# Batch 1's second product as seven half products, in a fused attention and mixer kernel on one core

## The chip, the core and the metric

The kernel runs on one core of a Trainium2 chip. Five engines work from queues of their own, each strictly in order: TensorE (PE in the profile; its weight loads are PEld), VectorE (DVE), ScalarE (ACT), GpSimd (POOL) and SyncE (SP), which only issues transfers. A semaphore holds an instruction, and with it all that stands behind it on its engine, until others are done. The metric is the device time of one execution in microseconds (us); lower is better.

## The reference

```python
q_p, k_p = phi(q), phi(k)             # relu(x) times cos and sin of the position, side by side
kv = einsum('bhsf,bhsd->bhfd', k_p, v);  z = k_p.sum(axis=2)
x  = (q_p @ kv) / (q_p . z + 1e-6)    # per head; heads joined: 8 batches x 576 x 512
u  = x + (x.T @ U @ V).T              # U 576x32, V 32x576, along the sequence
out = u + relu(u @ w_ch1) @ w_ch2     # w_ch1 512x2048, w_ch2 2048x512
```

q, k, v have 8 batches, 8 heads, 576 positions and 64 features; output is float32. The products run in bf16 with float32 sums in PSUM.

## The kernel before

The 576 positions of a batch are 4 chunks (c = 0 to 3) of 128 and a tail of 64; the tails of two batches (a pair, pr) make one chunk, cc=4. The first product u @ w_ch1 is done for 16 tiles j of 128 hidden columns: `g1_main` (L570) does four matmuls of 512 columns into one PSUM bank (g_ps), and ScalarE's relu (L589) writes `hid[b][:, j]`. `g1_tail` (L712) does the same for a tail chunk.

The second product has two forms. `g2_part` (L737) takes one chunk: 16 matmuls of 512 columns in four parts of four into one bank (o_ps, L762), then one VectorE add of u (L772) and a store. `half_part` (L865) takes two chunks, n and n+2, with the 2048 x 512 weights cut into four quarters `W2` (L796): instead of eight products of quarters it does seven (k = 0 to 6, product numbers in `ORDER`), each 8 matmuls of 256 columns into half a bank (h_ps, L894). It needs sums of hidden blocks made by `hid_sum` (L823, VectorE, L836; the fourth is done right after product 2) and sums of weight quarters made by `w2_sum` (L801, VectorE, L807, eight half sums). In the form "with g" the products alternate with units of a first product; in the form "alone", before this change used for batch 7 only, ScalarE copies products 1, 5, 6 and 4 out of PSUM (L912 to L920), VectorE adds products 2, 3 and 7 (L850), and GpSimd adds u and the copies (L921, L924).

The order is written out by hand. `slots` is a list of TensorE pieces; `put(at, f)` (L1346) hangs work behind slot `at`, and the loop at L1553 runs slot by slot, so that each engine's queue follows this order. Slots 0 to 15 are the first product of batch 0, 16 to 31 the second product of its four chunks, 32 to 47 the first product of batch 1, 48 to 51 the first product of the tail of batches 0 and 1, 52 to 55 the second product of that tail, 56 to 71 the second product of batch 1's four chunks (cc = 5 to 8) and 72 to 87 the first product of batch 2. The attention of batch b is hung in by `attention_plan` (L1007) around a slot w in `PLAN` (L998): q and k preparation (`q_prep`, `k_prep`), transpositions of q issued by SyncE (`qtr_dma`, L392), `kv_unit` (L340) at w and w+2, the five `x_unit` or `x_two` (L416, L1293: matmuls, a reciprocal and scalings) from w+4, `A_unit` and `u_mm` (L446, L476: the product with U and V), four `u_add` (L484, j = 0 to 3) and transpositions of u (`utr_dma`, L522). For batches 1 and 3, x_two has its scaling done by eight ScalarE copies (L1314).

PSUM has eight banks: X takes two, T one, and g0, g1, g2, o0, o1 one each. `Banks` (L55) deals them out in turn: tag "g" from g0, g1, g2, tag "o" from o0, o1, whoever asks next. `spare(at)` (L989) says which tag a piece of attention takes in a slot: "o" from 32 to 51, "g" from 52 on, and from 72 or 88 on other ones. Half products take banks from `ring` (L838), `bank(i)` being the i-th after `turn`. A piece that is given a bank waits until what was last written there has been read.

Stores of batch 0 and 1 that would crowd SyncE's queue are kept in `late` (L735) and issued behind slots 65 and 92 (L1551).

Of the kernel before, what the change touches and what calls it, by code (L numbers as in the profile page):

```python
# [17 lines left out]
def kernel(  # L18
# [53 lines left out]
    ps = Banks()  # L72
# [62 lines left out]
    V_, A_, G_ = nc.vector, nc.scalar, nc.gpsimd  # L135
# [599 lines left out]
    late = {}  # L735

    def g2_part(pr, cc, part, half=None):  # L737

        last = pr == NPAIR - 1 and cc == 4
        if part == 0 and not half or last and part == 3:  # L740
            if pr > 0:
                o_ps[pr, cc] = tail_bank()
            else:
                tag, bufs = ("g", 3) if 2 <= cc < 4 else ("o", 2)
                o_ps[pr, cc] = ps.tile([P, DM], FP32, tag=tag, bufs=bufs, name="o_ps")
        o = o_ps[pr, cc]
        if cc == 4:
            b, lhs, c = None, hid_tl[pr], 0
            u = u_tl[pr].rearrange("p (j n) -> p j n", n=P)
        else:  # L750
            b, c = (2 * pr, cc) if cc < 4 else (2 * pr + 1, cc - 5)
            lhs, u = hid[b], u_bf[b][:, :, c, :]

        if last:
            cols = slice(0, 384) if part < 3 else slice(384, DM)
            js = (range(0, 5), range(5, 10), range(10, NJ), range(NJ))[part]
        else:
            cols, js = slice(0, DM), range(part * 4, part * 4 + 4)
            if half is not None:
                js = js[2 * half : 2 * half + 2]  # L760
        for j in js:
            nc.tensor.matmul(  # L762
                out=o[:, cols],
                lhsT=lhs[:, j, c * P : c * P + P],
                rhs=w2_bf[:, j, cols],
                start=(j == 0),
                stop=(j == NJ - 1),
            )
        if js[-1] < NJ - 1:
            return  # L770
        o_sb = pool.tile([P, DM], FP32, tag="o_sb", bufs=8, name="o_sb")
        nc.vector.tensor_tensor(  # L772
            out=o_sb[:, cols].rearrange("p (j n) -> p j n", n=P),
            in0=u[:, cols.start // P : cols.stop // P, :],
            in1=o[:, cols].rearrange("p (j n) -> p j n", n=P), op=ALU.add,
        )
        eng = nc.gpsimd if pr < NPAIR - 1 else nc.scalar if part == 3 and last else nc.sync
        if pr == 0 and cc < 8:
            eng = nc.sync

        def store():
            if cc == 4:
                tail_store(eng, pr, o_sb, cols)
                return
            eng.dma_start(
                out=out[b].rearrange("(m k) n -> m k n", k=9)[:, c : c + 6 : 5, cols],
                in_=o_sb[:, cols],
            )

        if pr == 0 and cc < 7:  # L790
            late.setdefault(92 if 0 < cc < 5 else 65, []).append(store)
            return
        store()

# [6 lines left out]
    def w2_sum(n, half):  # L801

        a, b = (
            (W2[1], W2[0]), (W2[3], w2_s[0]), (W2[3], W2[1]), (W2[2], w2_s[1])
        )[n]
        js = slice(4 * half, 4 * half + 4)
        V_.tensor_tensor(  # L807
            out=w2_s[n][:, js], in0=a[:, js], in1=b[:, js], op=ALU.subtract
        )
# [28 lines left out]
    ring, turn = ["o0", "o1"], [0]  # L838
# [148 lines left out]
    ORD = (4, 0, 1, 2, 3)  # L987

    def spare(at):  # L989
        if at < 72:  # L990
            return ("o", 2) if 32 <= at < 52 else ("g", 3)
        return ("o", 2) if at < 88 else ("s", 1)

# [1 line left out]
    QORD = (4, 0, 1, 2, 3)  # L997
    PLAN = {  # L998
        2: (46, -15, V_, V_, -10, (-5, -4, -1)),
        3: (64, -12, V_, A_, -7, (3, 3, 18)),  # L1000
        4: (100, (-20, 1, V_, V_), (-13, 2, A_, V_), -12, (-9, -4, -4)),
        5: (127, (-24, 2, A_, A_), (-14, 2, A_, V_), (-14, -8, -5), (-8, -4, -4)),
        6: (157, (-23, 2, A_, A_), (-14, 2, A_, V_), (-14, -8, -6), (-8, -4, -4)),
        7: (189, (-24, 2, A_, A_), (-14, 2, A_, V_), (-12, -10, -8), ()),
    }

    def attention_plan(b):  # L1007

        plan = []
        if b < 4:  # L1010
            w, f_at, q_eng, k_eng, qtr, lo = PLAN[b]
        else:
            w, q_at, k_at, qtr, lo = PLAN[b]

        def put(at, f, *a, tag=False):
            if tag:
                a = a + spare(w + at)
            plan.append((w + at, lambda: f(b, *a)))

        for n, c in enumerate(QORD):  # L1020
            if b > 3:
                put(q_at[0] + q_at[1] * n, q_prep, c, q_at[2:])
                put(k_at[0] + k_at[1] * n, k_prep, c, k_at[2:])
                put(k_at[0] + (3 * n) // 2, v_prep, 0, H, (c,), (G_,))
                continue
            if b == 3:
                q_eng, k_eng = V_ if n == 3 else A_, A_ if n < 3 else None
                put((-12, -11, -10, -7, -3)[n], q_prep, c, (q_eng, q_eng))
                put(n - 9 if n < 3 else -5, k_prep, c, (A_, k_eng))
                if n > 2:  # L1030
                    put(2 * n - 12, k_prep, c, (None, V_))
                put(-4 if n > 2 else -6, v_prep, 0, H, (c,), (A_ if n > 2 else G_,))
                continue
            put(f_at + ((n - 1) % 5 if b == 2 else n), q_prep, c, (q_eng, q_eng))
            put(f_at + 6 + n, k_prep, c, (k_eng, k_eng))
            put((-6, -2, -1, -5, -5)[n], v_prep, 0, H, (c,), (V_ if n > 2 else A_,))
        for n, (c0, c1) in enumerate(((4, 5), (0, 2), (2, 4))):
            at = qtr[n] if b > 4 else 1 if b == 3 and n == 2 else qtr + 2 * n
            put(at, qtr_dma, c0, c1)
        plan.append((w + (b == 2), lambda: kv_unit(b, 0, *spare(w), A_ if b > 2 else V_)))  # L1040
        plan.append((w + 2, lambda: kv_unit(b, 1, *spare(w + 2), A_ if b > 2 else V_)))
        for n, c in enumerate(ORD):
            if b > 3:
                put((3 if b == B - 1 else 4) + 2 * n, x_unit, c, "X", 1)
            elif n % 2:
                put(9 if (b, n) == (3, 3) else 4 + (3 * n) // 2, x_two, c, tag=True)
            else:
                put(4 + (3 * n) // 2, x_unit, c, "X", 1)
        a_at = 15 - b if b < 4 else 14
        if b == B - 1:  # L1050
            put(a_at, A_unit, "s", 1, A_)
        else:
            put(a_at, A_unit, tag=True)
        odd = b % 2 == 1


        def two(at):
            return [T1, ("s", 1)] if at >= 88 else [spare(at)] * 2

        if b == B - 1:  # L1060
            plan.append((w + a_at + 2, lambda: u_mm(b, ("s", 1), js=(0, 1, 2))))
            plan.append((w + a_at + 5, lambda: u_mm(b, js=(3,))))
        else:
            plan.append((w + a_at + 2, lambda: u_mm(b, *two(w + a_at + 2))))
        for j in range(4):
            put(a_at + 2 + j + (2 if b > 4 and j > 1 else 0), u_add, j)
        put(a_at + 3, utr_dma, 0, 2)
        put(a_at + (7 if b > 4 else 5), utr_dma, 2, 4)
        if odd:
            if b == B - 1:  # L1070
                plan.append((w + a_at + 9, lambda: u_tail(b // 2, ("s", 1), js=(0, 1, 2))))
                plan.append((w + a_at + 11, lambda: u_tail(b // 2, js=(3,))))
            else:
                at = w + a_at + (10 if b == 5 else 9)
                plan.append((at, lambda at=at: u_tail(b // 2, *two(at))))
            put(a_at + (11 if b > 4 else 10), utr_dma, 4, 5)
        for at, t in zip(lo, loads(b + 1) if lo else ()):
            plan.append((w + at, t))
        return plan
# [44 lines left out]
    T1 = ("T", 1)  # L1124
# [219 lines left out]
    slots, todo = [], {}  # L1344

    def put(at, thunk):  # L1346
        todo.setdefault(at, []).append(thunk)

    def sums(b, n, ats):
        for i, at in enumerate(ats):  # L1350
            put(at, lambda i=i: hid_sum(b, n, i + 1))
# [24 lines left out]

    slots += [g1_second] + [g1(1, j) for j in range(1, NJ)]
    tail_slots(0)
    slots += [lambda cc=cc, p=p: g2_part(0, cc, p) for cc in range(4, 9) for p in range(4)]
    slots += [g1(2, j) for j in range(NJ)]  # L1380
    put(len(slots) - 1, lambda: ps.give("g", ("g0", "g1")))
    alone = len(slots)
# [147 lines left out]
    put(at - 2, lambda: tail_store(nc.sync, 3, o_last(1), slice(0, 512)))  # L1530
    put(at - 1, lambda: tail_store(A_, 2, o_last(0), slice(256, 512)))
    for n in range(8):
        put((44, 45, 49, 50, 65, 66, 75, 77)[n], lambda n=n: w2_sum(n // 2, n % 2))
    for j, ts_ in beside.items():
        todo[j] = list(ts_) + todo.get(j, [])

# [11 lines left out]
    for b in range(2, B):  # L1548
        for at, t in attention_plan(b):
            put(at, t)  # L1550
    for n in (65, 92):  # L1551
        put(n, lambda n=n: [store() for store in late[n]])
    for i, s in enumerate(slots):  # L1553
        s()
# [33 lines left out]
```

## Time and profile before

| what | value |
|---|---|
| median of three runs | 292.93 us (292.7 to 292.99) |
| the profiled execution: its time | 292.63 us |
| its span, first to last instruction | 290.9 us |
| granted TensorE clock | 0.997 |
| VectorE, ScalarE, GpSimd busy | 71%, 58%, 20% of the span |

The profile is of one execution. A row of a timeline gives start, length, engine, line, operation, output<-input and count, and in brackets how long the engine was idle before it and what ended that. A row of a group gives busy time and the mean length of one in ns. Matmuls overlap, so a row of several ends some 0.17 us after the next may start.

### The profile page before, as it was taken

To read this page: it belongs to the slowest core of one execution; us is meant where nothing else is said; L and a number is where in the kernel's file an instruction comes from. 1 tells how busy PE (TensorE), PEld (TensorE's weight loads), DVE (VectorE), ACT (ScalarE), POOL (GpSimd) and SP (SyncE) were. 2 spreads that over 40 slices of the span, in tenths; PEclk is the share of its full clock that TensorE was granted. 3 is DMA by queue.
4 is the path that set the end of the run, shared out by engine and by line. 5 is a ranking of instruction groups with operands and counts; after the bars stand their busy time and mean duration, and the time that the engine had idled before them with its cause. 6 is when DMAs were issued, how large, how long until landed. Compare 5 with 4: busy or idle time off the path is not lost.

```text
span 290.9 us, 7344 instructions
## 1 busy us (share of the span) xinstructions
PE 285.6 (98%) x2944; PEld 194.5 (67%) x2944; DVE 207.2 (71%) x503; ACT 169.2 (58%) x353; POOL 57.2 (20%) x91
## 2 busy tenths in 40 slices
PE   8999999999999999999999999999999999999994
PEld 3775564446645545776767666766777889889883
DVE  5977766496876687748647695679968787775773
ACT  2955752167881867578735864497654556657310
POOL 6420500000020002310500411024101222403330
PEclk9999999999999999999999999999999999999998
DMA  6999999999998999999599929994850964436023
GB/s 225 300 254 251 269 156 214 218 307 228 365 153 133 309 272 250 231 308 295 146 208 269 284 55 243 192 331 106 168 88 5 127 132 87 85 97 133 14 88 132
DMA packets 93126, 56.18 MB, mean 193 GB/s; under 512 B 56580, under 2 KB 89732, under 8 KB 93092
## 3 DMA queue, kind: packets, MB, share of 16 engines
q1 hardware_dynamic: 82452, 44.20, 61.7%
q0 software_dynamic: 10448, 11.31, 19.6%
q8 instruction: 23, 0.38, 0.5%
q10 hardware_dynamic: 192, 0.20, 0.2%
q14 instruction: 11, 0.09, 0.1%
HBM read 36.86 MB, written 9.44 MB: 159 GB/s over the span
## 4 chain that ended last, share of the span: by engine, by line
PE 92%; DMA 3%; SPq 2%; DVE 1%; issue 0%; ACT 0%; DVEq 0%; ACTq 0%
PE h_ps L894 28%; PE g_ps L580 27%; PE o_ps L762 8%; PE c_ps L677 6%; PE gt_ps L722 5%; DMA vst<-in_v_dram 3%; PE w_ps L235 3%; PE kv_ps L348 3%; PE x_ps L423 3%; PE a_ps L446 1%; PE h_ps L762 1%; PE va_ps L476 1%; PE t_ps L366 1%; PE t_ps L378 1%; SPq L522 1%; DVE u_bf L484 1%
## 5 line engine op out<-in xcount | busy, mean ns | idle before, releaser
L580 PE MATMUL g_ps<-uT,w_bf 128*128 128x512 bf16 x402 | 97.4, 379 | 0.1
L589 ACT ACTIVATE hid<-g_ps 128x512 bf16<-128x512 f32 x104 | 61.0, 599 | 56.9 <-PE g_ps L580 56.3
L580 PEld LDWEIGHTS <-w_bf 128*128 128x128 bf16 x402 | 37.7, 98 | 34.7 <-issue 0.4
L894 PEld LDWEIGHTS <-hid 128*128 128x128 bf16 x480 | 45.5, 98 | 9.6 <-issue 0.3
L894 PE MATMUL h_ps<-w_bf,hid 128*128 128x256 bf16 x288 | 37.1, 273 | 0.0
L762 PE MATMUL o_ps<-w_bf,hid 128*128 128x512 bf16 x128 | 30.1, 379 | 0.0
L894 PE MATMUL h_ps<-w_s,S 128*128 128x256 bf16 x208 | 26.5, 273 | 0.0
L894 PE MATMUL h_ps<-w_s,hid 128*128 128x256 bf16 x192 | 24.9, 273 | 0.0
L850 DVE TENSOR_TENSOR o_sb<-o_sb,h_ps 128x256 f32<-128x256 f32 (+1 forms) x36 | 15.5, 433 | 12.3 <-PE h_ps L894 10.1
L894 PEld LDWEIGHTS <-S 128*128 128x128 bf16 x208 | 20.1, 98 | 4.4
L953 POOL DMA_DIRECT2D out_dram<-o_sb x16 | 10.1, 631 | 63.5 <-DVE o_sb L850 49.3
L484 DVE TENSOR_TENSOR u_bf<-x_bf,va_ps 128x512 bf16<-128x512 bf16 x27 | 17.6, 680 | 6.4 <-PE va_ps L476 2.7
L132 POOL CAST v_ext<-vst 128x512 bf16<-128x512 f32 (+1 forms) x22 | 15.4, 729 | 32.4 <-DMA vst<-in_v_dram 29.6
L850 DVE TENSOR_TENSOR o_sb<-u_bf,h_ps 128x256 f32<-128x256 bf16 x28 | 11.7, 416 | 13.2 <-PE h_ps L894 13.1
L612 DVE TENSOR_TENSOR hid<-kept,c_ps 128x256 bf16<-128x256 f32 x36 | 14.7, 417 | 8.3 <-ACT kept L130 4.6
L762 PEld LDWEIGHTS <-hid 128*128 128x128 bf16 x128 | 11.5, 98 | 12.2
L130 ACT ACTIVATE kept<-c_ps 128x256 f32<-128x256 f32 x36 | 12.6, 385 | 7.3 <-PE c_ps L677 7.2
L952 POOL DMA_DIRECT2D o_sb<-u_bf x8 | 10.4, 1302 | 30.0 <-DVE rec L414 15.3
L722 PE MATMUL gt_ps<-uT_tl,w_bf 128*128 128x128 bf16 x256 | 16.2, 219 | 0.0
L433 DVE TENSOR_TENSOR x_bf<-x_ps,rec 128x512 bf16<-128x512 f32 x22 | 15.2, 691 | 0.8
L722 PEld LDWEIGHTS <-w_bf 128*128 128x128 bf16 x256 | 15.1, 98 | 0.7
L307 ACT ACTIVATE k_p<-kst,cosw 128x512 bf16<-128x512 f32 x20 | 14.2, 713 | 0.1
(190 smaller groups left out, 456.6 us busy)
## 6 DMA issues: line engine op xcount, KB each, us to landing
qst<-in_q_dram SPq DMA_DIRECT2D x14, 512.0 KB, 5.5
kst<-in_k_dram SPq DMA_DIRECT2D x12, 512.0 KB, 6.8
vst<-in_v_dram SPq DMA_DIRECT2D x10, 512.0 KB, 7.8
out_dram<-o_sb POOLq DMA_DIRECT2D x18, 256.0 KB, 4.0
out_dram<-o_sb SPq DMA_DIRECT2D x17, 256.0 KB, 2.7
w_bf<-in_moe_w_ch_dram POOLq DMA_DIRECT2D x7, 512.0 KB, 13.6
kst<-in_k_dram SPq DMA_DIRECT2D x4, 640.0 KB, 7.3
o_sb<-u_bf POOLq DMA_DIRECT2D x8, 256.0 KB, 3.6
```

The source lines that it names most:

```text
L132: eng.tensor_copy(out=o, in_=i)
L307: nc.scalar.activation(out=o, in_=i, func=AF.Relu, bias=0.0, scale=w)
L433: nc.vector.tensor_tensor(out=x_of(b, c, rows).rearrange("p (g i d) -> p g i d", g=2, d=D), in0=view[:, :, :, 0:D], in1=rec[rows].unsqueez ...
L484: nc.vector.tensor_tensor(out=u_bf[b][:, j, :, :], in0=x_bf[b][:, :, ns], in1=va[b][j].rearrange("p (c n) -> p c n", c=4), op=ALU.add,)
L580: nc.tensor.matmul(out=g_ps.rearrange("p (c t) -> p c t", c=4), lhsT=w1_bf[:, d, j * P : j * P + P], rhs=uT[b][:, d, :, :], start=(d == 0) ...
L589: nc.scalar.activation(out=hid[b][:, j, :], in_=g_ps, func=AF.Relu, bias=0.0, scale=1.0)
L612: V_.tensor_tensor(out=o, in0=x, in1=y, op=op)
L677: nc.tensor.matmul(out=w[to].rearrange("p (c t) -> p c t", c=2), lhsT=lhs[:, d, cs], rhs=rhs[:, d], start=(first and d == 0), stop=(d == 1 ...
L722: nc.tensor.matmul(out=g_ps[:, jj, :], lhsT=w1_bf[:, d, j * P : j * P + P], rhs=uT_tl[pr][:, d, :], start=(d == 0), stop=(d == 3),)
L762: nc.tensor.matmul(out=o[:, cols], lhsT=lhs[:, j, c * P : c * P + P], rhs=w2_bf[:, j, cols], start=(j == 0), stop=(j == NJ - 1),)
L850: eng.tensor_tensor(out=o, in0=x, in1=y, op=ALU.add)
L894: nc.tensor.matmul(out=acc, lhsT=lhs[:, j, :], rhs=rhs[:, j, :], start=(j == 0 and at is not None), stop=(j == 7), skip_group_check=at is ...
```

## The change

Batch 1's second product uses seven half products for each of its two chunk pairs (0, 2) and (1, 3), form "alone": 14 slots (56 to 69) for 16, so that all later slots have a number lower by two. Behind slot 55, `banks_of` leaves tag "g" two banks, g0 and g1, and gives the ring o0, o1, g2, starting at o0; behind slot 69 it is undone. The sums of batch 1's hidden blocks are made behind slots 47 to 53, and the weight sums behind slots 21 to 32 instead of 44 to 77. Entries of `PLAN` for batches 3 to 7, the limits in `spare` and `two` and the slots of late stores move along. The cast of batch 2's kv goes from VectorE to ScalarE. Batch 1's stores are now those of `half_store`, on GpSimd.

```diff
-        if pr == 0 and cc < 8:
+        if pr == 0:
             eng = nc.sync
...
-        if pr == 0 and cc < 7:
-            late.setdefault(92 if 0 < cc < 5 else 65, []).append(store)
+        if pr == 0:
+            late.setdefault(90 if cc else 60, []).append(store)
             return
...
     def spare(at):
-        if at < 72:
+        if at < 70:
             return ("o", 2) if 32 <= at < 52 else ("g", 3)
-        return ("o", 2) if at < 88 else ("s", 1)
+        return ("o", 2) if at < 86 else ("s", 1)
...
-        3: (64, -12, V_, A_, -7, (3, 3, 18)),
-        4: (100, (-20, 1, V_, V_), (-13, 2, A_, V_), -12, (-9, -4, -4)),
+        3: (63, -12, V_, A_, -7, (3, 3, 17)),
+        4: (98, (-20, 1, V_, V_), (-13, 2, A_, V_), -12, (-9, -4, -4)),
...
-        plan.append((w + (b == 2), lambda: kv_unit(b, 0, *spare(w), A_ if b > 2 else V_)))
-        plan.append((w + 2, lambda: kv_unit(b, 1, *spare(w + 2), A_ if b > 2 else V_)))
+        plan.append((w + (b == 2), lambda: kv_unit(b, 0, *spare(w), A_)))
+        plan.append((w + 2, lambda: kv_unit(b, 1, *spare(w + 2), A_)))
...
-    slots += [lambda cc=cc, p=p: g2_part(0, cc, p) for cc in range(4, 9) for p in range(4)]
+    slots += [lambda p=p: g2_part(0, 4, p) for p in range(4)]
+    sums(1, 0, (47, 48, 49))
+    sums(1, 1, (50, 51, 53))
+
+    def banks_of(g, o):
+        ps.give("g", g)
+        ring[:], turn[0] = o, 0
+
+    put(len(slots) - 1, lambda: banks_of(("g0", "g1"), ["o0", "o1", "g2"]))
+    for n in range(2):
+        for i7 in range(7):
+            slots.append(lambda n=n, i7=i7: half_part(1, n, i7, "alone"))
+        for i in range(2):
+            put(len(slots) - 1 + i, lambda n=n, i=i: half_store(1, n, i))
+    put(len(slots) - 1, lambda: banks_of(("g0", "g1", "g2"), ["o0", "o1"]))
...
     for n in range(8):
-        put((44, 45, 49, 50, 65, 66, 75, 77)[n], lambda n=n: w2_sum(n // 2, n % 2))
+        put((21, 22, 24, 26, 25, 31, 31, 32)[n], lambda n=n: w2_sum(n // 2, n % 2))
...
-    for n in (65, 92):
+    for n in (60, 90):
         put(n, lambda n=n: [store() for store in late[n]])
```

More of the change, by code (lines that the diff above doesn't have):

```diff
@@ L999 @@
         2: (46, -15, V_, V_, -10, (-5, -4, -1)),
-        3: (64, -12, V_, A_, -7, (3, 3, 18)),
-        4: (100, (-20, 1, V_, V_), (-13, 2, A_, V_), -12, (-9, -4, -4)),
-        5: (127, (-24, 2, A_, A_), (-14, 2, A_, V_), (-14, -8, -5), (-8, -4, -4)),
-        6: (157, (-23, 2, A_, A_), (-14, 2, A_, V_), (-14, -8, -6), (-8, -4, -4)),
-        7: (189, (-24, 2, A_, A_), (-14, 2, A_, V_), (-12, -10, -8), ()),
+        3: (63, -12, V_, A_, -7, (3, 3, 17)),
+        4: (98, (-20, 1, V_, V_), (-13, 2, A_, V_), -12, (-9, -4, -4)),
+        5: (125, (-24, 2, A_, A_), (-14, 2, A_, V_), (-14, -8, -5), (-8, -4, -4)),
+        6: (155, (-23, 2, A_, A_), (-14, 2, A_, V_), (-14, -8, -6), (-8, -4, -4)),
+        7: (187, (-24, 2, A_, A_), (-14, 2, A_, V_), (-12, -10, -8), ()),
     }
@@ L1057, in two @@
         def two(at):
-            return [T1, ("s", 1)] if at >= 88 else [spare(at)] * 2
+            return [T1, ("s", 1)] if at >= 86 else [spare(at)] * 2
         if b == B - 1:
```

## The prediction

> **What bounds the kernel now.** I read the page first (busy shares, the chain that ended last), then the chain in order of time, then TensorE's and VectorE's timelines from 36 to 113 us, where every edit lands, then the groups by shape for prices.
>
> ```profile
> span 290.9 us, 7344 instructions
> ...
> PE 285.6 (98%) x2944; PEld 194.5 (67%) x2944; DVE 207.2 (71%) x503; ACT 169.2 (58%) x353; POOL 57.2 (20%) x91
> ...
> PE 92%; DMA 3%; SPq 2%; DVE 1%; issue 0%; ACT 0%; DVEq 0%; ACTq 0%
> ```
>
> TensorE (PE) is busy for 98% of the span and holds 92% of the chain: whatever shortens its work is gained, and whatever makes it wait is lost at full size, since nothing behind it has slack. A busy share does not say at which rate it works, so I take the rate from the chain in order of time (start, length, what):
>
> ```profile
> 88.25 1.73 PE o_ps L762 x8
> ...
> 268.73 18.35 PE h_ps L894 x168
> ```
>
> Eight 512-column matmuls take 1.73 us, 0.216 each. The same seven-product form that the change brings to batch 1 ran at the end of this kernel as 168 matmuls of 256 columns in 18.35 us, 0.109 each and without a gap. So half the columns cost half the time, and the form itself can run at full rate.
>
> **The work removed and added.** Batch 1 had 4 chunks x 16 matmuls: 64 x 0.216 = 13.8 us. It gets 2 pairs x 7 products x 8 = 112 x 0.109 = 12.2 us. That is -1.6 us on the engine that sets the end, if it never waits. Whether it waits is decided by PSUM banks, and there the change hands over banks in a way that the old order did not.
>
> **The first wait: bank o0.** Counting the allocations with tag "o" from slot 47: first half of kv of batch 2 takes o1, the second o0, the upper half of x_two o1, the tail chunk's o_ps (slots 52 to 55) o0. Then banks_of restarts the ring at o0, and the first half product of slot 56 wants o0, which TensorE has just filled and VectorE must first empty (L772). Before, the next chunk took o1, long free. TensorE and VectorE around that point:
>
> ```profile
> 44.15 0.43 PE L423 MATMUL x_ps<-kv,q_pT 128*128 128x65 bf16 x8
> ...
> 77.65 1.03 PE L762 MATMUL o_ps<-w_bf,hid_tl 128*128 128x512 bf16 x4
> 78.51 1.03 PE L762 MATMUL o_ps<-w_bf,hid 128*128 128x512 bf16 x4
> 79.38 0.42 PE L423 MATMUL x_ps<-kv,q_pT 128*128 128x65 bf16 x8
> 79.64 2.75 PE L762 MATMUL o_ps<-w_bf,hid 128*128 128x512 bf16 x12
> 82.32 0.24 PE L446 MATMUL a_ps<-x_tl,U_bf 128*32 128x128 bf16 x4
> ...
> 82.71 1.90 PE L762 MATMUL o_ps<-w_bf,hid 128*128 128x512 bf16 x8
> 84.55 0.40 PE L476 MATMUL va_ps<-A_sb,V_bf 32*128 32x128 bf16 x16
> 84.88 2.76 PE L762 MATMUL o_ps<-w_bf,hid 128*128 128x512 bf16 x12
> 87.48 0.28 PE L348 MATMUL kv_ps<-v_ext,k_p 128*128 128x65 bf16 x4
> ...
> 88.08 1.89 PE L762 MATMUL o_ps<-w_bf,hid 128*128 128x512 bf16 x8
> ...
> 92.14 0.42 PE L423 MATMUL x_ps<-kv,q_tlT 128*128 128x65 bf16 x8
> ...
> 95.50 1.89 PE L580 MATMUL g_ps<-uT,w_bf 128*128 128x512 bf16 x8
> ```
>
> ```profile
> 43.40 0.69 DVE L433 TENSOR_TENSOR x_bf<-x_ps,rec 128x512 bf16<-128x512 f32 x1
> ...
> 48.09 1.88 DVE L484 TENSOR_TENSOR u_bf<-x_bf,va_ps 128x512 bf16<-128x512 bf16 x3 [2.35 <-PE side L476]
> ...
> 52.46 0.69 DVE L772 TENSOR_TENSOR o_sb<-u_bf,o_ps 128x512 f32<-128x512 bf16 x1 [1.89 <-PE o_ps L762]
> ...
> 57.62 0.49 DVE L309 TENSOR_SCALAR q_p<-qst,cosw 128x512 bf16<-128x512 f32 x1 [1.88 <-DMA qst<-in_q_dram]
> ...
> 66.05 0.43 DVE L132 CAST v_ext<-vst 128x512 bf16<-128x512 f32 x1 [0.43 <-DMA vst<-in_v_dram]
> ...
> 73.59 0.16 DVE L413 TENSOR_SCALAR rec<-x_ps 64x8 f32<-64x8 f32 x1 [0.41 <-PE x_ps L423]
> ...
> 76.73 0.17 DVE L413 TENSOR_SCALAR rec<-x_ps 128x8 f32<-128x8 f32 x1 [0.54 <-PE x_ps L423]
> ...
> 79.26 0.68 DVE L772 TENSOR_TENSOR o_sb<-u_tl,o_ps 128x512 f32<-128x512 bf16 x1
> ...
> 84.98 1.28 DVE L484 TENSOR_TENSOR u_bf<-x_bf,va_ps 128x512 bf16<-128x512 bf16 x2 [1.14 <-PE va_ps L476]
> ...
> 92.60 0.17 DVE L413 TENSOR_SCALAR rec<-x_ps 64x8 f32<-64x8 f32 x1 [0.43 <-PE x_ps L423]
> ```
>
> TensorE is done with the tail chunk at 78.51; VectorE emptied it from 79.26 to 79.94, late because the normalization of batch 2's x stands ahead of it in its queue. A handover from VectorE to TensorE shows at 43.40: the add ends at 44.09 and TensorE goes on at 44.15, so 0.06. Even with nothing added the wait is 79.94 + 0.06 - 78.51 = 1.5 us. The change also puts batch 1's sums (L836) into that queue, two pairs of three:
>
> ```profile
> L836 DVE TENSOR_TENSOR hid<-hid 128x1024 bf16<-128x1024 bf16 x12 | 8.9, 739 | 0.0
> ...
> L836 DVE TENSOR_TENSOR S<-hid 128x1024 bf16<-128x1024 bf16 x12 | 8.7, 722 | 2.3 <-ACT hid L589 2.2
> ...
> L836 DVE TENSOR_TENSOR S<-S,hid 128x1024 bf16<-128x1024 bf16 x12 | 8.2, 687 | 0.2
> ...
> L807 DVE TENSOR_TENSOR w_s<-w_bf,w_s 128x1024 bf16<-128x1024 bf16 x4 | 2.6, 682 | 0.0
> ...
> L850 POOL TENSOR_TENSOR o_sb<-o_sb,u_bf 128x512 f32<-128x512 f32 x2 | 2.3, 1155 | 11.9 <-ACT o_sb L130 11.9
> ...
> L850 DVE TENSOR_TENSOR o_sb<-o_sb,h_ps 128x512 f32<-128x512 f32 x2 | 1.4, 682 | 0.5 <-PE h_ps L894 0.5
> ```
>
> ```profile
> 68.87 1.18 ACT L589 ACTIVATE hid<-g_ps 128x512 bf16<-128x512 f32 x2
> ...
> 94.25 1.75 ACT L1314 ACTIVATE x_bf<-x_ps,rec 128x64 bf16<-128x64 f32 x8 [3.23 <-DVE rec L413]
> ```
>
> The first sum needs ScalarE's last relu of batch 1 (68.87 + 1.18 = 70.05). Four sums (0.72 + 0.69 + 0.74 + 0.72 = 2.87) end at 72.9, before the reciprocal of 73.59 could start: covered, in the place of kv casts and w_ch2 sums that leave. The other two, 0.69 and 0.74, follow later; 0.54 is taken up by the idle time before 76.73, and neighbouring rows overlap by some 0.08 each, which leaves 0.7. The add then runs 79.96 to 80.64 and TensorE goes on at 80.7: **2.2 us of waiting**; bounds 1.5 (sums hidden) and 2.9 (both in full).
>
> **The second and third wait: banks g1 and g0 for kv of batch 3.** banks_of also leaves tag "g" only g0 and g1. u_mm of batch 2 (slot 61) fills X, g1, g0; kv of batch 3 (slots 63 and 65) wants g1, then g0. They come free with u_add j=2 and j=3. Between those adds VectorE now has the new evacuations, and its queue is strict: the j=1 and j=2 adds stand behind the 128x512 add of product 7 (slot 62), which waits for that product and for GpSimd's add. TensorE from 80.7: product 1 0.87, x 0.26 (79.38 to 79.64), products 2, 5, 6 2.61, A 0.39 (82.32 to 82.71), products 4, 3 1.74, u_mm 0.33 (84.55 to 84.88), product 7 0.87: 87.77; one product more, and it wants kv at 88.64. VectorE: 87.77 + 0.17 until the last matmul is through (78.68 at the end of one row against 78.51 at the start of the next) + 0.68 less 0.08, + 1.28 for two adds (row 84.98), + 0.06: 89.9. GpSimd's add, 1.16, starts after ScalarE's copy of product 4, which stands behind preparations of batch 3, and may come up to 0.8 later than product 7. I take 90.1, **1.5 us**; bounds 1.2 and 2.0. Then kv 0.60 (87.48 to 88.08), products 2 and 5 1.74: 92.5; g0 comes free after VectorE's add of product 2 and u_add j=3, at 91.6 + 0.2 + 0.34 + 0.68 + 0.06 = 92.9: **0.4 us**, 0.3 to 0.7.
>
> **The fourth wait: g1 again.** x_two of batch 3 (slot 68) puts its upper half into g1; the second unit of batch 2's first product (slot 71) wants it. ScalarE's eight scalings free it: 94.25 to 96.00 before, 3.9 after x of c=4 began at 92.14. By the steps above that x begins at 95.2, one 0.34 add of product 3 stands between, so the scalings end at 99.4; TensorE is there at 98.6: **0.9 us**, 0.3 to 1.3 (there was one such bank more before, and no wait).
>
> **What costs nothing.** The sums of w_ch2 (8 x 0.68) move into VectorE's idle time ahead of 48.09, 52.46 and 57.62 (2.35, 1.89, 1.88); the one in slot 32 delays q and k preparation by 0.65, of which the 0.43 before 66.05 takes most; SyncE's q transpositions of batch 2 start 0.65 later. Cover gone, that is 0.2 to 0.6 in x of batch 2. The kv cast moves to ScalarE, idle there. Removing w_ch2 sums from 67 to 101 us frees VectorE where TensorE did not wait: no gain. Three stores of batch 1 move from SyncE to GpSimd, and those of batch 0 by two to five slots; nothing on the chain waits for a store. Plan entries moved by two keep their place against the slots. On SyncE one transposition comes later than its neighbours:
>
> ```profile
> 90.05 3.15 SPq L392 DMA_TRANSPOSE q_pT<-q_p x1
> ```
>
> ```profile
> 97.23 0.42 PE L1304 MATMUL x_ps<-kv,q_pT 128*128 128x65 bf16 x8
> ```
>
> It stands behind the transposition of u that waits for u_add j=3 (92.85), so it starts near 94.1 and is issued by 97.3; x_two of slot 72 then needs it at 97.23 + 3.1 = 100.3. Its lead after the issue shrinks from 4.0 to 3.0; 0, at most 0.7 (inside the upper bound of the fourth wait).
>
> **Sum.** -1.6 + 2.2 + 1.5 + 0.4 + 0.9 = +3.4; counted along TensorE's queue (second unit of batch 2 at 99.5 against 96.4) +3.1, because 0.25 of small gaps was in the old stretch. I take +3.3 on the profiled execution's 292.63 (span 290.9 and 1.7 around): 295.9. The runs' median lies 0.3 above that execution: 296.2. Lower bounds: -1.6 + 3.3 = +1.7, 294.6; upper: -1.6 + 6.9 = +5.3, 298.2.
>
> **Rivals.** (a) The change does what its arithmetic says, faster: -1.6, 291.3. Mechanism: the four waits shrink below 1.6 in all, which needs VectorE to empty o0 at once and GpSimd and VectorE to be done with product 7 before kv. Against it: the 1.5 floor of the first wait alone comes from rows that do not depend on the new sums, and the queue order fixes 1.2 more. 0.05. (b) Only the bank o0 costs, and waits two to four vanish because the first has given VectorE time: -1.6 + 2.2 = +0.6, 293.5. Against it: they hang on VectorE work that starts after TensorE's own products, so a delay of TensorE delays both. 0.07. (c) TensorE's waits bring its clock down.
>
> ```profile
> L580 PE MATMUL g_ps<-uT,w_bf 128*128 128x512 bf16 x402 | 97.4, 379 | 0.1
> ...
> L235 PE MATMUL w_ps<-zero 128*128 128x512 bf16 x20 | 7.0, 517 | 1.2 <-DVE zero L142 1.2
> ```
>
> At the start, the 20 matmuls L235 took 517 ns against 379 later, 2.8 us in all; one such slow stretch would give 296.2 + 2.8 = 299.0. The longest wait that I count, 2.2, is followed by 7 us of work. 0.04. The Trainium skill, "TensorE: Matmul & The Clock Gate", Part 1, says that the clock halves after an idle window of about 3.4 us; by it a wait of 2.2 keeps full clock, and no run here shows a gap that long in mid-kernel.
>
> **How the numbers follow.** My forecast has 0.84: 294.6 to 298.2 by its bounds. (b) lies below, (c) above; with (a) these are 0.16, so the range reaches only a little lower, 294.3 to 298.3. What a measurement tells from no change is 0.2%, 0.6 us: faster is (a), 0.05; (b) lies on that bound and is shared, same 0.04; slower 0.91.
>
> **What would show it.** TensorE rows: a gap of about 2 us between L762 hid_tl and the first L894 near 78.5, ended by VectorE's L772; gaps of 1.5 and 0.4 before the two groups of kv near 88 and 92; one before the second g_ps unit near 98.6, ended by ScalarE. The 112 matmuls L894 at 0.109. From there to the end the same spacing as before. Wrong would be: L894 following L762 within 0.5 us, kv groups without gaps, or a later stretch (113 to 291 us) that is shorter or longer than before by over 0.5.

## The result, and the profile after

The changed kernel takes 296.23 us (median of 4 runs, 296.13 to 296.52) against 292.81 for the kernel before beside it (292.47 to 292.99): ratio 1.012, 95% interval 1.010 to 1.014. It is slower, by 3.4 us. Its profiled execution took 296.13 us, against 292.63 for that of before: +3.5.

The page of the changed kernel, its span and the busy shares of the engines:

```profile
span 294.4 us, 7466 instructions
...
PE 284.8 (97%) x2992; PEld 199.2 (68%) x2992; DVE 211.7 (72%) x511; ACT 172.7 (59%) x363; POOL 63.7 (22%) x98
```

TensorE is busy 0.8 us less than before and the span is 3.5 us longer: the engine that sets the end stands still more. (It is 0.8 and not the 1.6 of the removed work because the last 0.17 us of a matmul, which the next one otherwise covers, stand alone ahead of each of five waits.) Where, the chain in order of time tells, by three landmarks that both kernels have (the tail of a pair's first product, gt_ps). First the kernel before, then the changed one:

```profile
71.52 1.79 PE gt_ps L722 x32
...
140.70 3.73 PE gt_ps L722 x64
...
207.28 1.79 PE gt_ps L722 x32
```

```profile
71.50 1.79 PE gt_ps L722 x32
...
144.64 3.73 PE gt_ps L722 x64
...
211.06 1.79 PE gt_ps L722 x32
...
272.51 18.36 PE h_ps L894 x168
```

Up to 71.5 nothing has changed, though the sums of w_ch2 lie there now. From the first landmark to the second it is 69.18 us before and 73.14 after: all of the loss, +3.96, lies in this stage. The next stretch is 0.16 shorter (66.58, 66.42), the one to the last half products the same (61.45 in both), what follows them 0.28 shorter. This stage length is used for all runs below, since it leaves out the start, which varies from one execution to the next: the first landmark lies between 71.07 and 72.55 us in the profiles of this document. For the same reason rows of two runs are compared by their distance from that landmark.

The waits of TensorE over the whole changed kernel (who waits, for whom, total us, times, longest):

```profile
PE h_ps L894 <- DVE o_sb L772: 1.9, 1, 1.9
PE kv_ps L348 <- DVE u_bf L484: 1.5, 2, 1.3
PE w_ps L235 <- DVE zero L142: 1.2, 1, 1.2
PE g_ps L580 <- ACT hid L589: 0.7, 1, 0.7
PE g_ps L580 <- ACT x_bf L1314: 0.7, 1, 0.7
```

Only the third, at the very start, is also in the kernel before. The same waits in TensorE's timeline of the changed kernel:

```profile
77.64 1.02 PE L762 MATMUL o_ps<-w_bf,hid_tl 128*128 128x512 bf16 x4
80.53 1.03 PE L894 MATMUL h_ps<-w_bf,hid 128*128 128x256 bf16 x8 [1.86 <-DVE o_sb L772]
81.40 0.42 PE L423 MATMUL x_ps<-kv,q_pT 128*128 128x65 bf16 x8
...
87.84 1.04 PE L894 MATMUL h_ps<-w_bf,hid 128*128 128x256 bf16 x8
90.14 0.28 PE L348 MATMUL kv_ps<-v_ext,k_p 128*128 128x65 bf16 x4 [1.26 <-DVE u_bf L484]
...
91.61 1.04 PE L894 MATMUL h_ps<-w_s,S 128*128 128x256 bf16 x8
92.89 0.28 PE L348 MATMUL kv_ps<-v_ext,k_p 128*128 128x65 bf16 x4 [0.24 <-DVE u_bf L484]
...
98.36 0.42 PE L423 MATMUL x_ps<-kv,q_pT 128*128 128x65 bf16 x8
99.45 0.81 PE L580 MATMUL g_ps<-uT,w_bf 128*128 128x512 bf16 x3 [0.67 <-ACT x_bf L1314]
...
113.28 1.04 PE L580 MATMUL g_ps<-uT,w_bf 128*128 128x512 bf16 x4
115.00 1.24 PE L580 MATMUL g_ps<-uT,w_bf 128*128 128x512 bf16 x5 [0.69 <-ACT hid L589]
```

The bracket counts from the end of the last matmul, some 0.17 us after the next could have started. Counted from start to start, as the prediction counts (four matmuls of 512 columns or eight of 256 are 0.87, x 0.26), the gaps are 80.53 - 78.51 = 2.02, 90.14 - 88.71 = 1.43, 92.89 - 92.48 = 0.41, 99.45 - 98.62 = 0.83 and 115.00 - 114.14 = 0.86 us: 5.55 in all. With the 1.6 us of work saved that makes +3.95 for the stage; it is +3.96. The half products themselves run at 0.87 for eight (80.53 to 81.40), 0.109 each.

The fifth gap was not foreseen. Behind slot 69 the change gives tag "g" its three banks again and restarts the count at g0. Batch 2's first product has 16 units, so that the 16th takes g0; then the old line behind it gives ("g0", "g1") and restarts at g0 again. Units 16 and 17 want the same bank one after the other, and the second waits for ScalarE's relu of the first. Before, the 16th unit had g1.

VectorE in the changed kernel, at the first two waits:

```profile
74.61 0.67 DVE L836 TENSOR_TENSOR S<-S,hid 128x1024 bf16<-128x1024 bf16 x1
...
76.69 0.68 DVE L836 TENSOR_TENSOR hid<-hid 128x1024 bf16<-128x1024 bf16 x1
...
79.80 0.68 DVE L772 TENSOR_TENSOR o_sb<-u_tl,o_ps 128x512 f32<-128x512 bf16 x1
...
88.11 0.69 DVE L850 TENSOR_TENSOR o_sb<-o_sb,h_ps 128x512 f32<-128x512 f32 x1 [0.37 <-POOL o_sb L850]
88.72 1.28 DVE L484 TENSOR_TENSOR u_bf<-x_bf,va_ps 128x512 bf16<-128x512 bf16 x2
```

The tail chunk's add ends at 80.48 and TensorE goes on at 80.53. Product 7's add is held by GpSimd, and the two u_adds that free g1 stand behind it, to 90.00; kv starts at 90.14.

### The profile page after: what moved, and what is told of

Its sections match the earlier page's. It is cut to its first block, busy times and chain, and to the rows that moved or that the text cites. A ratio compares the mean times of both kernels' runs of the same rounds, so it can differ in the third digit from the quotient of the medians.

```text
span 294.4 us, 7466 instructions
## 1 busy us (share of the span) xinstructions
PE 284.8 (97%) x2992; PEld 199.2 (68%) x2992; DVE 211.7 (72%) x511; ACT 172.7 (59%) x363; POOL 63.7 (22%) x98
## 4 chain that ended last, share of the span: by engine, by line
PE 94%; DVE 4%; ACT 1%; issue 1%; DVEq 0%
PE h_ps L894 31%; PE g_ps L580 30%; PE c_ps L677 6%; PE gt_ps L722 5%; PE o_ps L762 4%; PE w_ps L235 3%; PE kv_ps L348 3%; PE x_ps L423 2%; PE a_ps L446 1%; PE h_ps L762 1%; PE g_ps L597 1%; PE va_ps L476 1%; PE t_ps L366 1%; PE t_ps L378 1%; DVE u_bf L484 1%
## 5 line engine op out<-in xcount | busy, mean ns | idle before, releaser
L894 PEld LDWEIGHTS <-hid 128*128 128x128 bf16 x560 | 52.9, 98 | 12.7 <-issue 2.1
L894 PE MATMUL h_ps<-w_bf,hid 128*128 128x256 bf16 x336 | 43.3, 273 | 1.9 <-DVE o_sb L772 1.9
L894 PE MATMUL h_ps<-w_s,S 128*128 128x256 bf16 x240 | 30.4, 272 | 0.0
L894 PE MATMUL h_ps<-w_s,hid 128*128 128x256 bf16 x224 | 29.0, 273 | 0.0
L894 PEld LDWEIGHTS <-S 128*128 128x128 bf16 x240 | 23.1, 98 | 4.7
L953 POOL DMA_DIRECT2D out_dram<-o_sb x20 | 12.7, 636 | 62.4 <-DVE o_sb L850 48.7
L850 DVE TENSOR_TENSOR o_sb<-u_bf,h_ps 128x256 f32<-128x256 bf16 x32 | 13.3, 416 | 16.3 <-PE h_ps L894 16.2
L130 ACT ACTIVATE o_sb<-h_ps 128x256 f32<-128x256 f32 x24 | 9.2, 381 | 11.1 <-PE h_ps L894 9.3
L762 PE MATMUL o_ps<-w_bf,hid 128*128 128x512 bf16 x64 | 15.0, 379 | 0.0
L413 DVE TENSOR_SCALAR rec<-x_ps 128x8 f32<-128x8 f32 (+2 forms) x39 | 6.2, 159 | 12.0 <-PE x_ps L423 9.6
```

Source lines behind the costliest of these rows:

```text
L130: nc.scalar.activation(out=o, in_=i, func=AF.Copy, bias=0.0, scale=1.0)
L762: nc.tensor.matmul(out=o[:, cols], lhsT=lhs[:, j, c * P : c * P + P], rhs=w2_bf[:, j, cols], start=(j == 0), stop=(j == NJ - 1),)
L850: eng.tensor_tensor(out=o, in0=x, in1=y, op=ALU.add)
L894: nc.tensor.matmul(out=acc, lhsT=lhs[:, j, :], rhs=rhs[:, j, :], start=(j == 0 and at is not None), stop=(j == 7), skip_group_check=at is ...
```

## The experiments

The theory: the loss is five waits of TensorE for PSUM banks that the change hands over in a new order. The rivals: the new work on VectorE and ScalarE, or the form of the products, costs the time wherever the banks are. All runs in one table; the ratio is to the kernel before on the same chip, and "stage" is the stretch between the first two landmarks in the run's profile (69.18 before, 73.14 after).

| run | median us (lowest to highest, runs) | ratio, 95% interval | stage us |
|---|---|---|---|
| e1 ring | 296.1 (295.71 to 297.96, 4) | 1.0115, 1.0074 to 1.0157 | 72.32 |
| e2 kv in T | 295.61 (295.12 to 296.63, 5) | 1.0093, 1.0061 to 1.0125 | 72.19 |
| e3 order of g | 294.65 (294.2 to 296.06, 8) | 1.0065, 1.0042 to 1.0087 | 71.46 |
| e4 all three | 297.01 (295.13 to 298.55, 4) | 1.0131, 1.0077 to 1.0185 | 72.53 |
| e5 sums later | 296.43 (295.93 to 297.12, 4) | 1.0117, 1.0089 to 1.0144 | 72.97 |
| e6 w_ch2 sums alone | 292.5 (292.02 to 293.63, 10) | 0.9991, 0.9972 to 1.0009 | 69.19 |
| e7 bank alone | 294.23 (293.44 to 294.82, 10) | 1.0037, 1.0021 to 1.0054 | 70.66 |
| e8 e4, kv cast by VectorE | 294.75 (293.47 to 297.02, 10) | 1.0065, 1.0039 to 1.0091 | 72.45 |
| e9 e4, stores sooner | 292.82 (292.01 to 293.5, 12) | 1.0008, 0.9994 to 1.0022 | 69.68 |
| e10 e8, stores sooner | 292.63 (291.78 to 295.03, 12) | 1.0007, 0.9989 to 1.0026 | 68.64 |
| e11 e10, u_adds sooner | 292.01 (291.38 to 295.37, 12) | 0.9983, 0.9958 to 1.0009 | 68.58 |
| e12 e10, all u_adds first | 291.77 (291.04 to 293.55, 12) | 0.9981, 0.9963 to 0.9999 | 68.39 |

**Each bank alone: e1, e2, e3.** All start from the changed kernel.

```diff
 e1
-    put(len(slots) - 1, lambda: banks_of(("g0", "g1"), ["o0", "o1", "g2"]))
+    put(len(slots) - 1, lambda: banks_of(("g0", "g1"), ["g2", "o1", "o0"]))
 e2
-        plan.append((w + (b == 2), lambda: kv_unit(b, 0, *spare(w), A_)))
-        plan.append((w + 2, lambda: kv_unit(b, 1, *spare(w + 2), A_)))
+        kv_at = [T1] * 2 if b == 3 else [spare(w), spare(w + 2)]
+        plan.append((w + (b == 2), lambda: kv_unit(b, 0, *kv_at[0], A_)))
+        plan.append((w + 2, lambda: kv_unit(b, 1, *kv_at[1], A_)))
 e3
-    put(len(slots) - 1, lambda: banks_of(("g0", "g1", "g2"), ["o0", "o1"]))
+    put(len(slots) - 1, lambda: banks_of(("g2", "g0", "g1"), ["o0", "o1"]))
```

> Only the ring's order changes: g2, o1, o0, so that the first half product takes a bank that is long free and the tail chunk's o0 comes third. Bank theory: the gap of 2.02 us between the tail chunk and the first half product goes; VectorE's add of the tail chunk still ends near 80.5, when the third product wants o0, so 0 to 0.3 stays; the ScalarE copy of product 1 stands behind preparations until about 81.8 and may hold product 6 by up to 0.5. Time 294.3 to 295.0. VectorE theory (VectorE has too much to do there, whatever the banks): the wait only moves to the next piece that needs VectorE, time stays 296.0 to 296.4.

> Only kv of batch 3 changes its bank: T, free since 79, instead of g1 and g0 that wait for u_add. Bank theory: the gaps of 1.43 and 0.41 us ahead of the two kv groups go, 294.4 to 294.9; the fourth wait (ScalarE's scalings) may grow by a little. VectorE theory: the wait comes back at the products that follow, 296.0 to 296.4.

> Only the order in which batch 2's first product takes g2, g0, g1 changes. Bank theory: the gap before its second unit (0.83, ScalarE's scalings in g1) and the one before batch 3's first unit (0.7, the same bank g0 twice running) go: 294.7 to 295.0. If the scalings hold something else as well, 295.4 to 295.8. VectorE theory: no change, 296.2, since both waits are on ScalarE.

e3 came out as expected: waits four and five are gone, and the stage is 1.68 shorter, 0.83 + 0.86 = 1.69. In e1 and e2 the waits that were aimed at are gone too, so that the bank was their cause; but the stage gains only 0.82 of 2.02 and 0.95 of 1.84, and the times fall short of what was expected: e2's lies between the two ranges, and e1's 296.1 lies in that of the VectorE theory. What takes the rest in e1 can be read along its engines; ScalarE, GpSimd, VectorE and TensorE of e1:

```profile
84.97 1.15 ACT L130 ACTIVATE v_ext<-vst 128x512 bf16<-128x512 f32 x2
86.01 0.37 ACT L130 ACTIVATE o_sb<-h_ps 128x256 f32<-128x256 f32 x1
```

```profile
86.47 1.16 POOL L850 TENSOR_TENSOR o_sb<-o_sb,u_bf 128x512 f32<-128x512 f32 x1 [2.09 <-ACT o_sb L130]
```

```profile
87.66 0.69 DVE L850 TENSOR_TENSOR o_sb<-o_sb,h_ps 128x512 f32<-128x512 f32 x1 [0.58 <-POOL o_sb L850]
```

```profile
78.87 1.04 PE L894 MATMUL h_ps<-w_bf,hid 128*128 128x256 bf16 x8
...
84.97 1.05 PE L894 MATMUL h_ps<-w_bf,hid 128*128 128x256 bf16 x8 [0.42 <-DVE hid L836]
...
89.69 0.28 PE L348 MATMUL kv_ps<-v_ext,k_p 128*128 128x65 bf16 x4 [1.48 <-DVE u_bf L484]
```

Counted from the first landmark (71.87 in e1, 71.50 in the changed kernel), the first half product starts 2.03 us sooner than in the changed kernel (7.00, 9.03), kv of batch 3 only 0.82 (17.82, 18.64), because ScalarE has its preparation of batch 3 in front of the copy of product 4, GpSimd waits for that copy, VectorE for GpSimd, and the u_adds stand behind. TensorE, early now, waits for a hidden sum (0.42) and longer for kv. The waits are in series: the first one had given ScalarE time. In e2, which leaves the first wait in place, x of batch 3 waits 0.7 us for ScalarE's cast of kv, a wait that was hidden behind those of kv.

**All banks right, and a worse time: e4, e8.** e4 makes the three edits together; e8 also has VectorE empty the second half of kv:

```diff
-        plan.append((w + 2, lambda: kv_unit(b, 1, *kv_at[1], A_)))
+        plan.append((w + 2, lambda: kv_unit(b, 1, *kv_at[1], V_ if b == 3 else A_)))
```

> The three edits together. Bank theory: of 5.4 us of waits 0.5 to 1.5 stay (copies and adds that now come too late for a TensorE that does not wait), the 1.6 of the seven products are gained: 291.2 to 292.3, below the 292.8 of before. VectorE theory: 294.5 or more, since the queue of VectorE is as full as it was.

> e4 (all four banks set right) with one more edit: the second half of kv of batch 3 is emptied by VectorE instead of ScalarE. In e4 that cast started at 94.08, behind ScalarE's copy of a chunk that waited 5.05 us for an output store to land, TensorE waited 2.41 us for it, and the granted clock fell to 0.50 from about 94.3 to 97.5. If that queue was all that e4 had left, x of batch 3 starts without a wait, the clock stays at 1.00, and the time is 291.3 to 292.4, below the kernel before. If ScalarE's late copy then holds TensorE by the bank of its chunk instead, the time is 293.0 to 295.0 with a wait of the half products on ScalarE's o_sb.

e4 misses what the theory gave it by nearly 5 us, and its time falls to the rival; but all five waits are gone, and there is one of 2.4 us in their place, which neither had named. (The profile is of the fastest of e4's four executions; the others take 1.2 to 3.4 us longer at the same mean clock, and what they waited for is not shown.) ScalarE in e4, then in e8, and TensorE in e8:

```profile
93.80 0.38 ACT L130 ACTIVATE o_sb<-h_ps 128x256 f32<-128x256 f32 x1 [5.05 <-DMA out_dram<-o_sb]
94.08 0.38 ACT L130 ACTIVATE kv<-kv_ps 128x260 bf16<-128x260 f32 x1
```

```profile
94.80 0.38 ACT L130 ACTIVATE o_sb<-h_ps 128x256 f32<-128x256 f32 x1 [5.26 <-DMA out_dram<-o_sb]
```

```profile
92.40 0.42 PE L423 MATMUL x_ps<-kv,q_tlT 128*128 128x65 bf16 x8
95.24 1.86 PE L894 MATMUL h_ps<-w_bf,hid 128*128 128x256 bf16 x8 [2.41 <-ACT o_sb L130]
```

The copy of a product of the second pair needs an output buffer. There are eight (`bufs=8`); four still hold chunks of batch 0 whose stores are kept until slot 90, and the first pair has three, so that the copy waits until a store of the first pair, issued on GpSimd a few us earlier, has landed. In e4 the kv cast stands behind that copy, in e8 the bank of the copied product is wanted. The wait is the same, 2.41, by either way: the second branch of e8's expectation. In the changed kernel the same copy runs at 92.91, 0.26 us after its product has ended (91.61 + 1.04), because TensorE, held by the waits ahead of it, comes to that product 3 us later than in e4 (91.61, 88.58).

The eight matmuls of e8 at 95.24 took 1.86 us where such eight take 1.04. e8 by windows (each ends with the granted clock of TensorE, DMA share and GB/s):

```profile
94.00:96.00 2.00, 0.76 (x4) 0.55 (x4) 0.00 (x0) 0.94 (x3) 0.17 (x1) 0.81 1.22 255
96.00:98.00 2.00, 2.00 (x18) 1.49 (x16) 0.79 (x5) 0.06 (x1) 1.33 (x2) 0.50 1.10 250
98.00:100.00 2.00, 1.95 (x18) 1.31 (x18) 0.79 (x2) 1.77 (x9) 1.52 (x2) 0.84 0.86 212
```

The clock fell to 0.50 and came back; e4 shows the same (0.50 in the windows from 95 to 97 us). By the mean clock, not every execution has it. Of e8's ten, four have a mean granted clock of 0.992 or 0.993 and take 295.47 to 297.02 us, six have 0.998 or 0.999 and take 293.47 to 295.06: the fall costs some 1.9 us between the two means (296.1 and 294.2). All four of e4 have 0.992 or 0.993. So the rival (c) of the prediction exists, in another kernel than the one it was written for.

**The rest of the prediction's terms: e5, e6, e7.** e5 changes the changed kernel, e6 and e7 the kernel before.

```diff
 e5
-    sums(1, 1, (50, 51, 53))
+    sums(1, 1, (50, 59, 59))
 e6
-        put((44, 45, 49, 50, 65, 66, 75, 77)[n], lambda n=n: w2_sum(n // 2, n % 2))
+        put((21, 22, 24, 26, 25, 31, 31, 32)[n], lambda n=n: w2_sum(n // 2, n % 2))
 e7
+    put(55, lambda: ps.at.update(o=ps.at["o"] + 1))
     slots += [g1(2, j) for j in range(NJ)]
```

> The second pair's last two sums of batch 1's hid (2 x 0.68 us on VectorE) go behind slot 59 instead of slots 51 and 53. If the first wait is the tail chunk's add standing in VectorE's queue behind these sums as well as behind batch 2's normalization, the add starts near 79.3 instead of 79.80, the wait at bank o0 falls from 2.0 to about 1.5 us (the floor that the prediction took from the rows of before), and the time is 295.5 to 295.9. If the sums are covered by VectorE's idle time, the wait stays at 2.0 and the time at 296.2.

> The kernel before, with only the eight sums of w_ch2 moved to slots 21 to 32. The prediction puts this part at nothing: 292.5 to 293.2, the same as before, and the first 70 us of TensorE's rows unchanged. The rival, that the sums delay the normalization and preparation of batch 2 by 0.2 to 0.6 us, gives 293.1 to 293.5.

> The kernel before, computing everything as before, but with the count of the tag o moved on by one ahead of the chunk that follows the tail chunk, so that this chunk takes the bank o0 that the tail chunk has just filled. If the bank handover alone makes the first wait, TensorE stands 79.94 + 0.06 - 78.51 = 1.5 us behind the tail chunk until VectorE's add has run, and the time is 293.9 to 294.6 (the later chunks then take the other bank of the pair in turn, which can add some tenths). If the wait comes from the form of the new products or their sums and not from the bank, there is no such gap, and the time is 292.5 to 293.2.

e6: no change of the time, and a stage of 69.19 against 69.18. Its first landmark comes at 72.55, but by a wait of 1.41 us at 9 us, far ahead of the first sum that was moved; e3 has the like (1.27). e7, TensorE:

```profile
78.02 1.02 PE L762 MATMUL o_ps<-w_bf,hid_tl 128*128 128x512 bf16 x4
80.35 1.02 PE L762 MATMUL o_ps<-w_bf,hid 128*128 128x512 bf16 x4 [1.30 <-DVE o_sb L772]
```

80.35 - 78.02 - 0.87 = 1.46 us, and the stage is 1.48 longer: the old products in a wrong bank lose what the prediction gave as the floor of the first wait, 1.5, without any new work. e5, VectorE's tail add and TensorE:

```profile
79.64 0.68 DVE L772 TENSOR_TENSOR o_sb<-u_tl,o_ps 128x512 f32<-128x512 bf16 x1
```

```profile
80.36 1.03 PE L894 MATMUL h_ps<-w_bf,hid 128*128 128x256 bf16 x8 [1.30 <-DVE o_sb L772]
...
86.86 0.40 PE L476 MATMUL va_ps<-A_sb,V_bf 32*128 32x128 bf16 x16 [0.33 <-DVE A_sb L132]
```

This execution passes the first landmark 0.40 us later than that of the changed kernel, so that the add's 79.64 stands against 79.80 + 0.40 = 80.20. The wait fell from 1.86 to 1.30, as expected: two sums of VectorE were 0.56 of it. But 0.33 went into a new wait for VectorE, and the time did not follow: the stage is 0.17 shorter, and 296.43 lies above the expected 295.5 to 295.9.

**Undoing what e4 and e8 ran into: e9 to e12.** e9 (on e4) and e10 (on e8) store two more chunks of batch 0 with slot 60; e11 and e12 move batch 2's u_adds in e10 (e12 shown; e11 has `j // 2` for the 0).

```diff
 e9, e10
-            late.setdefault(90 if cc else 60, []).append(store)
+            late.setdefault(90 if cc > 2 else 60, []).append(store)
 e12
-            put(a_at + 2 + j + (2 if b > 4 and j > 1 else 0), u_add, j)
+            put(a_at + 2 + (0 if b == 2 else j) + (2 if b > 4 and j > 1 else 0), u_add, j)
...
-        put(a_at + (7 if b > 4 else 5), utr_dma, 2, 4)
+        put(a_at + (7 if b > 4 else 4 if b == 2 else 5), utr_dma, 2, 4)
```

> e4 (the four banks set right, kv of batch 3 cast by ScalarE) with two more of batch 0's output chunks stored with slot 60 instead of slot 90, so that the second chunk pair finds output buffers whose stores went out 5 us earlier. If the waiting copy in ScalarE's queue (5.05 us in e4 for a store to land) was what e4 and e8 had left, that wait falls under 1 us, TensorE has no gap over 0.5 us between 79 and 115 us, the clock stays at 1.00, and the time is 291.0 to 292.0: below the kernel before by up to the 1.6 us of work. If the stores, now ahead of the transpositions on SyncE, hold these up or land as late as before, TensorE still waits and the time is 292.8 to 295.0.

> The same two stores in slot 60 on e8 (second half of kv of batch 3 emptied by VectorE). By the same theory 291.0 to 292.0 and no wait of the half products on ScalarE's o_sb, 2.4 us in e8; equal to e9 if the place of the kv cast no longer matters once the buffers are free, which the theory says. By the rival 292.8 to 295.0.

The buffers were it: in e10 the copy waits 0.69 us, for its product, and TensorE for no bank over 0.21. The times fall to that of the kernel before, but 0.6 to 0.8 short of what was expected. e10's ScalarE, and its chain in order of time:

```profile
90.01 0.38 ACT L130 ACTIVATE o_sb<-h_ps 128x256 f32<-128x256 f32 x1 [0.69 <-PE h_ps L894]
```

```profile
86.24 1.17 POOL o_sb L850
...
91.16 4.05 DMA uT<-u_bf
...
95.25 0.59 PE g_ps L580 x2
```

The chain has left TensorE: it runs over GpSimd's add, VectorE and the transposition of u into batch 2's first product. e9 waits 1.1 us for the same transposition; why it waits longer than e10 stays open.

> e10 with batch 2's four u_adds in slots 61, 61, 62, 62 instead of 61 to 64, and the second transposition of u one slot sooner. In e10 the chain that ends last runs from GpSimd's add of the pair over VectorE's add of product 7, the last u_adds (to 90.24) and a transposition of 4.05 us to batch 2's first product at 95.25. If that chain is what e10 has left, the transposition ends 0.6 to 0.9 us earlier, the first product of batch 2 follows the last half product without a gap, and the time is 0.3 to 0.9 us below e10: 291.7 to 292.3, below the kernel before. If the rest of e10 lies elsewhere, the time stays within 0.2 us of e10's 292.6.

> The same with all four u_adds in slot 61, ahead of VectorE's add of product 7, into the 0.94 us that VectorE stood idle there in e10. By the theory the transposition starts near 89.0 instead of 91.2, more than TensorE can use, and the time is that of e11 (291.7 to 292.3); the add of product 7 comes some 0.9 us later, and if the bank that it frees is wanted at once, one wait of up to 0.9 us takes the gain back, 292.4 to 293.0.

e12, VectorE and TensorE:

```profile
85.46 2.48 DVE L484 TENSOR_TENSOR u_bf<-x_bf,va_ps 128x512 bf16<-128x512 bf16 x4
87.86 0.68 DVE L850 TENSOR_TENSOR o_sb<-o_sb,h_ps 128x512 f32<-128x512 f32 x1
```

```profile
93.20 1.03 PE L894 MATMUL h_ps<-w_s,hid 128*128 128x256 bf16 x8
94.08 1.03 PE L580 MATMUL g_ps<-uT,w_bf 128*128 128x512 bf16 x3
```

The first product follows the last half product at 0.88, without a gap. Both medians lie in the expected range, but the stage does not bear out a gain of 0.3 to 0.9 us over e10: in the one profiled execution of each it is 0.06 shorter in e11 and 0.25 in e12. In e10 TensorE loses 0.39 us to the transposition (94.51 - 93.55 - 0.87 and 95.68 - 94.51 - 0.87); in e11 that is gone, but the gap for a hidden sum has grown from 0.25 to 0.58. The intervals of e10, e11 and e12 overlap, so the times do not show a gain over e10 either. e12's median is 0.83 us below that of the kernel before (292.60 in that comparison), by the ratio 0.9981 it is 0.56, at the edge of what can be measured: its interval ends at 0.9999. Its stage of 68.39 is 0.79 below that of before, half of the 1.6 of work that the seven products save. Most of the other half stands in two waits of e12:

```profile
PE h_ps L894 <- DVE hid L836: 0.2, 1, 0.2
PE h_ps L894 <- ACT s_sb L130: 0.2, 1, 0.2
```

From start to start they are gaps of 84.04 - 82.78 - 0.87 = 0.39 and 81.42 - 80.19 - 0.87 = 0.36 us: a sum of hidden blocks that comes too late, and a copy of a product that ScalarE makes too late.

## Why the prediction was right

- Work, -1.6: right. The products run at 0.109. e12, with the five waits out, keeps half of the saving in its stage (0.79), and 0.75 stands in two new gaps.
- First wait, bank o0: 2.2 predicted, 2.02 measured. The add was to run from 79.96 to 80.64 and ran from 79.80 to 80.48. The bank is its cause (e1 without it, e7 with it and nothing else), VectorE's sums 0.56 of its length (e5; the prediction had 0.7).
- Second and third, g1 and g0: 1.5 and 0.4 predicted, 1.43 and 0.41 measured; kv was to start at 90.1 and 92.9, and did at 90.14 and 92.89. The step that carried it, the u_adds behind an add that waits for GpSimd, is in the VectorE rows after.
- Fourth, g1 behind ScalarE's scalings: 0.9 predicted, 0.83 measured.
- "From there to the end the same spacing as before" was wrong: the fifth wait, 0.86, at 114.1. The prediction followed each bank that is taken away and not the place where the count restarts and meets the next hand-over. The sign that the prediction named, a stretch from 113 us on that differs by over 0.5, does not catch it: the gap lies ahead of that stretch, which starts with batch 2's first half product at 112.80 before and 116.72 after and is 0.4 shorter (178.1, 177.7). The total stayed right in part by luck: against the fifth wait stand 0.31 by which the four others came out smaller than the 5.0 predicted, and 0.44 that came off behind the stage (0.16 and 0.28), whose cause stays open. That 296.23 meets 296.2 to 0.03 is luck too.
- The 0.25 of small gaps, taken off in one of the prediction's two counts: not borne out. The second unit of batch 2 came at 99.45 against 95.50 + 0.87 = 96.37, +3.08, and the four waits less the work are 4.69 - 1.6 = +3.09, so the new stretch has such gaps too.
- The sums of w_ch2 at nothing: right (e6).
- Rival (a), the waits vanish, and (b), only o0 costs: both fell with the rows of the second to fourth wait. Rival (c), the clock: not here, where the longest idle time of the four waits was 1.86 us, but in e4 and e8.
- Against rival (b) the prediction said that the later waits hang on work behind TensorE's own products, "so a delay of TensorE delays both". That holds only in part: in e1 TensorE comes 2.03 us sooner and kv only 0.82, and 1.2 of the first wait's 2.02 us come back later. The terms were right as a sum of what stands there, not as a list of what each would give back alone.

## What to carry to other kernels

Where banks or buffers are dealt out in turn, write down for each hand-over, and for each place where a count restarts, who had the bank last and when it is read empty; a work saving of 1.6 us was lost more than three times over in five such places. Waits of one stage are often in series: removing one shows the next queue (here ScalarE's preparation, output buffers held by late stores, a transposition), so a gain is to be expected only when the whole chain up to the next landmark has been followed. A wait that is much longer than the others can cost its length and then the clock: 2.41 us did in e4 and in some executions of e8, 1.86 did not in the changed kernel.

## What the runs showed of the hardware

The granted clock fell in mid-kernel while TensorE stood idle for 2.41 us (e4 and e8), and stayed at 0.50 for 3.42 us: in finer windows it is down from 94.30 to 97.72 in e4 and from 95.22 to 98.64 in e8. The falls come 2.2 and 2.4 us after the last matmul has ended (92.10 and 92.82). Half a clock over 3.42 us is 1.7 us of work, near the 1.9 that e8's executions with and without the fall lie apart. In the changed kernel 1.86 us of idle time left the clock at 1.00. One execution each of e1 (297.96 us), e10 (295.03) and e11 (295.37) also has a mean clock of 0.992 to 0.994, though the profiles of these kernels show no wait over 1.5 us; what brought it down there is not shown.

The Trainium skill, "TensorE: Matmul & The Clock Gate", Part 1, gives an idle window of about 3.4 us before the clock halves, about as much of busy time until it is full again, and calls the window free-running, so that the same kernel differs from run to run. The way back and the differing executions agree with e4 and e8. The way down does not: an idle time a full us shorter was enough, and in the 3.42 us ahead of the fall TensorE had still worked for 1.2 (e4) and 1.0 us (e8). So the prediction's sentence, that a wait of 2.2 us keeps full clock by that page, held here for the changed kernel's 1.86 but is no safe bound; no run here shows an idle time between 1.86 and 2.41 us.
